# Eleven layers of a first block in three matmul passes instead of one fp32 pass, with later attention splits and another last stretch

## The chip, the cores and the metric

The kernel runs on one core of one Trainium2 chip. The metric is the device time of one execution in microseconds (us). One execution was also taken by the hardware profiler; its span runs from the first to the last instruction. The engines are TensorE (PE, with its weight loads as PEld), VectorE (DVE), ScalarE (ACT), GpSimd (POOL) and SyncE (SP), which issues the transfers. Each engine takes its instructions in the program's order.

## The reference, cut to what matters

```python
for t in range(S):                                    # attention, 4 batches x 8 heads, 768 steps, width 48
    cur = np.einsum('bhd,bhe->bhde', u[None] * kt, vt)
    y[:, :, t] = np.einsum('bhd,bhde->bhe', rt, state + cur)
    state = wt[:, :, :, None] * state + np.einsum('bhd,bhe->bhde', kt, vt)
...
h = x @ w_in                                          # 3072 tokens, 384 -> 2048
x = (h * np.clip(h + 3.0, 0.0, 6.0) / 6.0) @ w_out    # 2048 -> 384
...
xn = x / np.sqrt(np.mean(x * x, axis=-1, keepdims=True) + 1e-06) * rms_g
out = (silu(xn @ w_gate) * (xn @ w_val)) @ w_out2     # 384 -> 1536 -> 384
```

## The kernel before

The 768 steps are cut into six blocks c of 128 steps; a block holds 512 tokens (four batches). For each block there are four attention jobs (one per batch; job j = 4c + b) and the 16 layers f of the first MLP, 128 hidden channels each. The program is a list of steps n, written out by hand. A step holds one `ff1` (a layer's first matmuls, L613) and the `ff2` of two steps earlier (L630). Block 0 has 21 steps: layers 0 to 4 are done in halves of 256 tokens in steps 0 to 9, layers 5 to 15 at the whole width of 512 tokens in steps 10 to 20, so layer f has step f + 5. Block 1 begins with step 21. The lists `before[n]`, `between[n]` and `behind[n]` hold what is emitted ahead of a step's `ff1`, after it, and at its end; this alone sets the order on each engine.

There are two ways to do a layer. In the fp32 way (L444 and L450) one fp32 matmul per 128x128 tile multiplies the unsplit weight and input; the profile shows it as two instructions. In the three-pass way (L438, L467) weight and input each have a high part (fp32r) and a low remainder, and three fp32r matmuls per tile do high x high, high x low of the input, low of the weight x high, in that order (`PASS`). In block 0, layers below `F32_F` = 12 take the fp32 way.

What a three-pass layer needs: `Weight.scale` (ACT L146) and `Weight.bits` (DVE L151 and L152, here the shift and the or) make the fp32 weight in a tile `x` (three buffers); a transfer copies it into its place in `wide_a` (layers 0 to 6) or `wide_b` (7 to 15); `Weight.parts` then writes the high part (ACT L161) and the low part (DVE L162). Behind `ff1`, `emit_act` runs ACT L455 and DVE L456 (the min and multiply, which frees one of two PSUM tiles `hps`, so `ff1` of step n + 2 waits for it), and `emit_split` runs ACT L460 and POOL L461, which reads one of two tiles `a`. In block 0 the parts of x itself (`x_parts`, tile `xt`) are made behind step 15.

An attention job of blocks 1 to 5 is placed by `plan(j, n)`: in step n two scans on DVE (L273) and a product on POOL (`bonus1`, L300 and L301); in n + 1 two DVE products (L296, `muls`), a reduce that waits for POOL (L305) and three small POOL instructions (`decay`); in n + 2 `fill` (eight ACT instructions, L331), the matmuls `aps` and DVE's `choose` (L356, which waits for the fill); in n + 3 the matmuls `yps` (which wait for `choose`), the copy `y` (ACT L398) and eight small transfers x<-y; in n + 5 `split` (ACT L414, POOL L415) into `xt` of the next block. In block 0 the jobs 4, 5, 6, 7 have n = 6, 9, 12, 15, and job 8 has n = 19.

The second MLP follows in three rounds of two blocks. At the very end the loop over `FLUSH` (L1117) gives the last five products e2 to e6 of the last group, one PSUM bank `pe` for all of them, with units F of output matmuls between them; `done` (L837) multiplies each by its gate.

Of the kernel before, what the change touches and what calls it, by code (L numbers as in the profile page):

```python
# [9 lines left out]
F32 = mybir.dt.float32  # L10
# [3 lines left out]
AF = mybir.ActivationFunctionType  # L14
ALU = mybir.AluOpType
# [14 lines left out]
WP = 4 * DM  # L30
NG = F2 // 3
LAGS = (5, 0, 0, 0, 0, 0)
F32_F = 12


@with_exitstack
def kernel(
# [93 lines left out]

    class Weight:
        def __init__(self, src):
            self.src, self.near = src, False

        def load(self):
            self.raw = st_p.tile([128, 2 * DM], U64, tag="raw", name="raw", bufs=3)
# [11 lines left out]
        def bits(self):  # L149
            x = st_p.tile([128, 2 * DM], U32, tag="x", name="x", bufs=3)  # L150
            nc.vector.tensor_scalar(x, self.words()[0], 29, None, ALU.logical_shift_right)  # L151
            nc.vector.scalar_tensor_tensor(  # L152
                out=x, in0=self.mag.bitcast(U32), scalar=3, in1=x, op0=ALU.logical_shift_left, op1=ALU.bitwise_or)
            self.x = x.bitcast(F32).rearrange("p (a n) -> p a n", a=2)
            nc.sync.dma_start(
                out=self.dst[:, :, 1, :].bitcast(U32), in_=x.rearrange("p (a n) -> p a n", a=2))
            if not self.near:
                self.x = self.dst[:, :, 1, :].bitcast(F32)

        def parts(self):  # L160
            nc.scalar.activation(out=self.dst[:, :, 0, :], in_=self.x, func=AF.Copy)  # L161
            nc.vector.tensor_tensor(  # L162
                out=self.dst[:, :, 1, :], in0=self.x, in1=self.dst[:, :, 0, :].bitcast(F32), op=ALU.subtract)


# [371 lines left out]
    def plan(j, n):  # L537

        jb = jobs[j]
        before[n] += [jb.scans, jb.bonus1]  # L540
        before[n + 1] += [jb.muls, jb.bonus2, jb.decay]
        before[n + 2] += [jb.fill]
        between[n + 2] += [jb.pe_a, jb.pe_kt, jb.choose, jb.copy_kt]
        between[n + 3] += [jb.pe_y, jb.pe_u, jb.copy_y, jb.add_u]
        if j + 2 < len(jobs):
            behind[n + 3] += [lambda: jobs[j + 2].load("w", "rk", "v")]
        if j + 1 < len(jobs):
            behind[n + 1] += [lambda: jobs[j + 1].load("rks")]
        before[n + 5] += [jb.split]


    j0, j1, j2, j3 = jobs[:B]
# [22 lines left out]
        if f + 3 < F1:  # L575
            behind[n] += [wa[f + 3].load]
    for f in range(F1):
        before[f + 19 if f < F32_F else f + LAGS[0] - 1] += [wa[f].parts]
    behind[2] += [lambda: jobs[4].load("w", "rk", "rks", "v")]
    behind[4] += [lambda: jobs[5].load("w", "rk", "v")]  # L580

# [6 lines left out]
    for c in range(1, NC_):  # L588
        norm_plan(c, first[c], False)

    def x_parts():
        for k in range(KT):
            h = xts[0][:, k, 0, :]
            nc.scalar.activation(out=h, in_=x0[:, k, :], func=AF.Copy)
            nc.vector.tensor_tensor(out=xts[0][:, k, 1, :], in0=x0[:, k, :], in1=h.bitcast(F32), op=ALU.subtract)

    behind[F32_F + LAGS[0] - 2] += [x_parts]
    acc, norms, todo = None, {}, []


# [41 lines left out]
    def run(fs):  # L642
        for x in fs:
            x()
# [85 lines left out]
    def after(n, *fns):  # L730
        for x in fns:
            queue.append([n, x])
# [27 lines left out]
    class Triple:  # L760
# [76 lines left out]
        def done(self, i, o, ps=None):  # L837
            src = o if ps is None else ps
            self.o[i] = o
            if self.gate is None:  # L840
                nc.scalar.activation(out=o, in_=src, func=AF.Silu)  # L841
                return
            eng = nc.gpsimd if ps is None else nc.vector
            eng.tensor_tensor(out=o, in0=src, in1=self.gate.o[i], op=ALU.mult)  # L844
            f, t = i // 2, i % 2

            def split():
                g = gset(self.j // 2 * 2 + t)[f]
                nc.scalar.activation(out=g[:, 0, :], in_=o, func=AF.Copy)
                nc.gpsimd.tensor_tensor(out=g[:, 1, :], in0=o, in1=g[:, 0, :].bitcast(F32), op=ALU.subtract)  # L850
            after(6 if self.fast else 2, split)

    class Plain(Triple):

# [111 lines left out]
    for f in range(W1):  # L966
        wa[f].dst = wpair[f]
        wa[f].near = f < 2
    run((j0.scans, j0.pairs, j0.pe_bonus, j0.muls, j0.fill, j0.pe_a, j1.scans, j1.pairs, j1.pe_bonus, j1.muls))
    run((j0.choose, j1.fill, j1.pe_a, j0.pe_y0, wa[0].scale, wa[0].bits, wa[3].load, j1.choose, j1.pe_y0))  # L970
    run((j0.copy_y0, wa[1].scale, wa[1].bits, wa[4].load, j1.copy_y0, j2.scans))
# [142 lines left out]
        count += 1  # L1114

    FULL = "b a1 e2 d c1 F F e3 c2 a2 F e4 c3 F F e5 c4 F F e6 c5 F F e1".split()
    FLUSH = "F e2 F e3 F F e4 F F e5 F e6 F F".split()  # L1117
    prev, gate, coming = None, None, None
    fill = ff2_units() + ff2_units()
    for j in range(6 * NG + 1):  # L1120
# [25 lines left out]
        if j < 4:  # L1146
            room = 8 if j else 18
            for i, x in enumerate(cur.units((1, 0) if j == 3 else (0, 1))):
                paced(x)
                if fill and i * room // 18 < (i + 1) * room // 18:  # L1150
                    paced(fill.pop(0))
            assert count == lengths[j]
            continue
        want, n = {4: 7, 5: 7, 6: 6}.get(j, 9), 0
        for u in FULL if cur else FLUSH:
            if u == "F":
# [17 lines left out]
            coming = None  # L1174
        prev = cur
    assert not chores, list(chores)
    for x in fill + out_units(NC_ // 2 - 1, NG - 1, 0, (0, 2, 1)):
        unit(x)
    for x in out_units(NC_ // 2 - 1, NG - 1, 1, (0, 1, 2), None, True):
        unit(x)  # L1180
# [81 lines left out]
```

## Time and profile before

| | |
|---|---|
| time, median of 3 runs | 954.37 us (954.22 to 954.45) |
| the profiled execution: time, span | 955.4 us, 953.6 us |
| PE busy | 932.0 us, 98% of the span |
| DVE, ACT, POOL busy | 641.8, 476.5, 539.8 us |
| block 0 from step 10 to block 1's first matmuls | 72.20 to 135.87 us |
| block 0, PE's begin of step 12 and of step 15 | 81.62 and 101.02 us |
| from step 10 to block 1: PE, DVE, ACT, POOL busy | 63.47, 50.20, 32.45, 22.71 us |

PE is busy almost throughout, so time is gained where PE's own work shrinks, and lost where PE is made to wait.

### The profile page before, as it was taken

How to read it: one execution, taken by the hardware profiler on the slowest of the kernel's cores; microseconds unless marked ns; L12 is line 12 of the kernel's file. 1: busy time of each engine (PE TensorE's matmuls, PEld its weight loads, DVE VectorE, ACT ScalarE, POOL GpSimd, SP SyncE). 2: the span in 40 equal slices, each digit the busy share in tenths (PEclk: the TensorE clock that was granted, in tenths of full speed). 3: DMA queues.
4: the chain of work that ended last, by engine and by line, in shares of the span. 5: the costliest groups of instructions: out<-in, count | busy, mean ns of one | idle time of the engine just before them, and what ended most of it. 6: DMA issues, size and time to landing. Idle time of an engine off the chain costs nothing.

```text
span 953.6 us, 14291 instructions
## 1 busy us (share of the span) xinstructions
PE 932.0 (98%) x5085; PEld 735.8 (77%) x5085; DVE 641.8 (67%) x908; ACT 476.5 (50%) x946; POOL 539.8 (57%) x459
## 2 busy tenths in 40 slices
PE   5899999999999999999999999999999999999998
PEld 4675577778878887777888888787777887888876
DVE  6867776878778787867645377557798557554543
ACT  3544656645655654564554554446545444433331
POOL 0022355766866676774465677579466679235325
PEclk9899999999999999999999999999999999999999
DMA  9687842236654563661662477854699642644321
GB/s 341 217 327 235 282 148 81 83 110 214 201 191 164 169 205 125 214 212 41 232 223 67 153 293 260 293 215 173 202 375 326 257 181 83 248 166 148 151 78 67
DMA packets 63127, 184.77 MB, mean 194 GB/s; under 512 B 8912, under 2 KB 23248, under 8 KB 58448
## 3 DMA queue, kind: packets, MB, share of 16 engines
q1 hardware_dynamic: 63056, 183.87, 54.7%
q8 instruction: 40, 0.66, 0.3%
q14 instruction: 31, 0.25, 0.1%
HBM read 134.29 MB, written 39.32 MB: 182 GB/s over the span
## 4 chain that ended last, share of the span: by engine, by line
PE 88%; DVE 5%; issue 2%; ACT 2%; POOL 1%; DMA 1%; SPq 0%; POOLq 0%; ACTq 0%; DVEq 0%
PE o L467 17%; PE hps L438 16%; PE o L744 14%; PE pe L744 10%; PE pc L744 8%; PE pa L744 4%; PE o L450 3%; PE hps L444 3%; PE pb L744 3%; PE aps L350 2%; PE yps L392 2%; PE pd L744 1%; PE ktp L338 1%; PE yps L386 1%; DVE w L273 1%
## 5 line engine op out<-in xcount | busy, mean ns | idle before, releaser
L461 POOL TENSOR_TENSOR g<-a,g 128x512 fp32r<-128x512 f32 x84 | 116.4, 1385 | 139.8 <-ACT g L460 139.7
L456 DVE SCALAR_TENSOR_TENSOR a<-a,hps 128x512 f32<-128x512 f32 x84 | 57.3, 682 | 83.8 <-ACT a L455 83.6
L467 PE MATMUL o<-g,wide_b 128*128 128x512 f32 x441 | 113.4, 399 | 0.0
L438 PE MATMUL hps<-xt,wide_b 128*128 128x512 f32 x441 | 111.9, 398 | 0.0
L744 PE MATMUL o<-xt,wide_b 128*128 128x512 f32 x405 | 107.5, 395 | 0.0
L455 ACT ACTIVATE a<-hps,half 128x512 f32<-128x512 f32 x84 | 57.4, 683 | 84.1 <-PE hps L438 79.9
L438 PEld LDWEIGHTS hps<-xt,wide_b 128*128 128x128 f32 x441 | 82.7, 187 | 21.2 <-issue 1.0
L467 PEld LDWEIGHTS o<-g,wide_b 128*128 128x128 f32 x441 | 81.2, 188 | 19.5 <-issue 0.5
L460 ACT ACTIVATE g<-a 128x512 fp32r<-128x512 f32 x84 | 53.1, 632 | 80.5 <-DVE a L456 78.8
L744 PEld LDWEIGHTS o<-xt,wide_b 128*128 128x128 f32 x405 | 76.0, 188 | 18.2
L467 PE MATMUL o<-g,wide_a 128*128 128x512 f32 x315 | 78.6, 394 | 0.0
L438 PE MATMUL hps<-xt,wide_a 128*128 128x512 f32 x315 | 77.6, 390 | 0.2 <-POOL xt L415 0.2
L273 DVE TENSOR_TENSOR_SCAN w<-w,dd 128x520 f32<-128x520 f32 x48 | 74.7, 1556 | 4.5 <-DMA w<-in_dram 2.9
L438 PEld LDWEIGHTS hps<-xt,wide_a 128*128 128x128 f32 x315 | 59.0, 188 | 13.3 <-POOL xt L415 0.6
L467 PEld LDWEIGHTS o<-g,wide_a 128*128 128x128 f32 x315 | 58.2, 188 | 12.3 <-issue 0.2
L779 DVE TENSOR_TENSOR q<-pc,q 128x512 f32<-128x512 f32 x80 | 55.1, 688 | 17.8 <-PE pc L744 7.0
L844 POOL TENSOR_TENSOR q<-q,q 128x512 f32<-128x512 f32 x40 | 55.2, 1380 | 14.5 <-DVE q L779 14.3
L331 ACT ACTIVATE a<-iperm,cb 128x128 f32<-128x128 f32 x192 | 58.5, 387 | 0.1
L744 PE MATMUL o<-g,wide_b 128*128 128x512 f32 (+1 forms) x216 | 55.5, 390 | 0.0
L300 POOL TENSOR_TENSOR rks<-rks 128x384 f32<-128x384 f32 x20 | 29.6, 1482 | 42.4 <-DMA rks<-in_dram 37.1
L841 ACT ACTIVATE q<-q 128x512 f32<-128x512 f32 x40 | 25.3, 632 | 51.3 <-DVE q L779 51.3
L844 POOL TENSOR_TENSOR o<-o,o 128x512 f32<-128x512 f32 x10 | 14.1, 1409 | 63.9 <-DVE o L779 63.9
(204 smaller groups left out, 2020.2 us busy)
## 6 DMA issues: line engine op xcount, KB each, us to landing
wraw<-in_dram SPq DMA_DIRECT2D x36, 384.0 KB, 4.0
wide_b<-wo SPq DMA_DIRECT2D x12, 1152.0 KB, 8.0
w<-wd SPq DMA_DIRECT2D x10, 1280.0 KB, 6.0
wide_b<-wd SPq DMA_DIRECT2D x10, 1280.0 KB, 6.0
w<-in_dram SPq DMA_DIRECT2D x24, 520.0 KB, 3.9
rk<-in_dram SPq DMA_DIRECT2D x24, 512.0 KB, 5.1
raw<-in_dram SPq DMA_DIRECT2D x16, 768.0 KB, 7.3
rks<-in_dram SPq DMA_DIRECT2D x20, 384.0 KB, 5.4
```

The lines of the kernel that those rows point to most:

```text
L273: nc.vector.tensor_tensor_scan(out=x, data0=x, data1=dd.rearrange("p a h j -> p (a h j)"), initial=0.0, op0=ALU.mult, op1=ALU.add)
L300: nc.gpsimd.tensor_tensor(out=x, in0=x, in1=self.rks[:, 1, :], op=ALU.mult)
L331: nc.scalar.activation(out=self.head(h), in_=iperm, func=AF.Copy, scale=self.cb[:, h, :])
L438: nc.tensor.matmul(ps, slot[:, l, k * 128:(k + 1) * 128], xt[:, k, r, :], start=(k == 0 and j == 0), stop=(k == KT - 1 and j == 2))
L455: nc.scalar.activation(out=a, in_=ps, func=AF.Relu, scale=1.0 / 6.0, bias=half)
L456: nc.vector.scalar_tensor_tensor(out=a, in0=a, scalar=1.0, in1=ps, op0=ALU.min, op1=ALU.mult)
L460: nc.scalar.activation(out=g[:, 0, :], in_=a, func=AF.Copy)
L461: nc.gpsimd.tensor_tensor(out=g[:, 1, :], in0=a, in1=g[:, 0, :].bitcast(F32), op=ALU.subtract)
L467: nc.tensor.matmul(acc[m][:, cols], slot[:, l, m * 128:(m + 1) * 128], g[:, r, :], start=(first and j == 0), stop=(parts or last and j == ...
L744: nc.tensor.matmul(ps, lhs[:, l, :], rhs[:, r, :], start=first and j == 0, stop=True, skip_group_check=not (first and j == 0))
L779: nc.vector.tensor_tensor(out=out, in0=a, in1=b, op=op)
L844: eng.tensor_tensor(out=o, in0=src, in1=self.gate.o[i], op=ALU.mult)
```

## The change

Layers 5 to 15 of block 0 all take the three-pass way (`F32_F` = 5, seven layers more). Their parts are made from the tile `x`, without the transfer into `wide_a` or `wide_b`, and stand first in a step shortly before the layer's `ff1`; for the layers in `LOW_POOL` the low part is POOL's. The parts of x are made behind steps 6, 7 and 8, the low ones on POOL. An attention job's `split` stands behind its step, but for the last job of a block. In the flush the F units stand two by two ahead of each product, the last ten units of output are taken from one list, and the last gate products are on DVE.

```diff
-F32_F = 12
+F32_F = 5
+LOW_POOL = (5, 6, 7, 9, 11, 13)
...
+            if self.stays:
+                return
             nc.sync.dma_start(
                 out=self.dst[:, :, 1, :].bitcast(U32), in_=x.rearrange("p (a n) -> p a n", a=2))
...
-        def parts(self):
+        def parts(self, pool=False):
             nc.scalar.activation(out=self.dst[:, :, 0, :], in_=self.x, func=AF.Copy)
-            nc.vector.tensor_tensor(
+            (nc.gpsimd if pool else nc.vector).tensor_tensor(
...
-        before[n + 5] += [jb.split]
+        (before if jb.b == B - 1 else behind)[n + 5] += [jb.split]
...
-        before[f + 19 if f < F32_F else f + LAGS[0] - 1] += [wa[f].parts]
+        if f < F32_F:
+            before[f + 19] += [wa[f].parts]
+        else:
+            before[{5: 6, 6: 8, 7: 9, 8: 11}.get(f, f + 4)].insert(0, lambda f=f: wa[f].parts(f in LOW_POOL))
...
-    behind[F32_F + LAGS[0] - 2] += [x_parts]
+    for k in range(KT):
+        behind[6 + k] += [lambda k=k: x_parts(k)]
...
-            eng = nc.gpsimd if ps is None else nc.vector
+            final = self.j == 6 * NG - 1
+            eng = nc.gpsimd if ps is None and not final else nc.vector
...
-            after(6 if self.fast else 2, split)
+            after(4 if final else 6 if self.fast else 2, split)
...
-    FLUSH = "F e2 F e3 F F e4 F F e5 F e6 F F".split()
+    FLUSH = "F F e2 F F e3 F F e4 F F e5 F F e6".split()
...
+        if not cur:
+            fill += out_units(NC_ // 2 - 1, NG - 1, 0, (0, 2, 1))
```

Line numbers shift by 3 to 7 in the changed kernel. On POOL, from job 4's product (L300, L301) to job 5's, there stands before:

```order
L300 TENSOR_TENSOR rks<-rks 128x384
L301 TENSOR_TENSOR rks<-rks,ub 128x384
L288 TENSOR_TENSOR g<-f_109,w 128x4
L289 TENSOR_TENSOR st_104<-st_104,g 128x192
L291 COPY f_109<-w 128x4
L300 TENSOR_TENSOR rks<-rks 128x384
L301 TENSOR_TENSOR rks<-rks,ub 128x384
```

and in the changed kernel, from behind job 4's product (here L303, L304) on:

```order
L600 TENSOR_TENSOR xt<-x_93,xt 128x512
L291 TENSOR_TENSOR g<-f_109,w 128x4
L292 TENSOR_TENSOR st_104<-st_104,g 128x192
L294 COPY f_109<-w 128x4
L600 TENSOR_TENSOR xt<-x_93,xt 128x512
L165 TENSOR_TENSOR wide_a<-x,wide_a 128x2x384
L600 TENSOR_TENSOR xt<-x_93,xt 128x512
L165 TENSOR_TENSOR wide_b<-x,wide_b 128x2x384
L303 TENSOR_TENSOR rks<-rks 128x384
L304 TENSOR_TENSOR rks<-rks,ub 128x384
```

Three low parts of x (128x512) and the low parts of layers 6 and 7 (128x768) stand between the two jobs; layer 5's stands ahead of job 4's product.

On ACT, from the L455 of step 12 to job 6's fill, there stands before:

```order
L455 ACTIVATE g<-hps,half 128x512
L398 ACTIVATE y<-yps 128x512
L146 ACTIVATE mag<-raw 128x768
L455 ACTIVATE g<-hps,half 128x512
L146 ACTIVATE mag<-raw 128x768
L414 ACTIVATE xt<-x 128x3x128
L331 ACTIVATE a<-iperm,cb 128x128 x8
```

and in the changed kernel:

```order
L458 ACTIVATE a<-hps,half 128x512
L463 ACTIVATE g<-a 128x512
L401 ACTIVATE y<-yps 128x512
L147 ACTIVATE mag<-raw 128x768
L164 ACTIVATE wide_b<-x 128x2x384
L458 ACTIVATE a<-hps,half 128x512
L463 ACTIVATE g<-a 128x512
L147 ACTIVATE mag<-raw 128x768
L164 ACTIVATE wide_b<-x 128x2x384
L334 ACTIVATE a<-iperm,cb 128x128 x8
```

Two splits (L463, each behind DVE's min and multiply of its step) and the high parts of layers 9 and 10 stand ahead of the fill now, and job 5's split (L414) stands behind step 14.

On PE, in the flush (`pe` is a product e2 to e6, `pa`, `pb`, `pc` and `o` are F units of three matmuls), there stands before:

```order
L744 MATMUL pe<-wide_b 128x512 x3
L744 MATMUL pa<-xt,wide_b 128x512 x3
L744 MATMUL pe<-wide_b 128x512 x3
L744 MATMUL pa<-xt,wide_b 128x512 x3
L744 MATMUL pe<-wide_a,wide_b 128x512 x3
L744 MATMUL pa<-xt,wide_b 128x512 x3
L744 MATMUL pb<-xt,wide_b 128x512 x3
L744 MATMUL pe<-wide_a,wide_b 128x512 x3
```

and in the changed kernel:

```order
L750 MATMUL pe<-wide_b 128x512 x3
L750 MATMUL pa<-xt,wide_b 128x512 x6
L750 MATMUL pe<-wide_b 128x512 x3
L750 MATMUL pa<-xt,wide_b 128x512 x3
L750 MATMUL pb<-xt,wide_b 128x512 x3
L750 MATMUL pe<-wide_a,wide_b 128x512 x3
```

Two units, where there was one, stand now between each product and the next.

## Rows read from the trace of the kernel before

**Rows 1.** Waits of PE, whole span: total us, times, longest us

```profile
PE yps L386 <- DVE a L356: 1.2, 2, 0.7
...
PE pe L744 <- DVE o L779: 0.6, 2, 0.4
```

**Rows 2.** The chain that ended last: start us, us, what, count

```profile
91.78 2.58 PE o L450 x6
...
195.07 2.10 PE hps L438 x9
...
238.42 2.04 PE o L467 x9
```

**Rows 3.** Timelines of PE and POOL where block 1 begins

```profile
135.87 2.11 PE L438 MATMUL hps<-xt,wide_a 128*128 128x512 f32 x8 [0.20 <-POOL xt L415]
...
134.08 1.73 POOL L415 TENSOR_TENSOR xt<-x,xt 128x384 fp32r<-128x384 f32 x1
```

**Rows 4.** Timeline of DVE in block 1

```profile
168.47 1.24 DVE L273 TENSOR_TENSOR_SCAN w<-w,dd 128x520 f32<-128x520 f32 x1
...
169.99 1.91 DVE L273 TENSOR_TENSOR_SCAN w<-w,dd 128x520 f32<-128x520 f32 x1
171.82 1.98 DVE L162 TENSOR_TENSOR wide_b<-wide_b 128x768 fp32r<-128x768 f32 x1
...
174.32 2.34 DVE L296 TENSOR_TENSOR rk<-rk,w 128x512 f32<-128x512 f32 x2
```

**Rows 5.** Timeline of POOL in the same stretch

```profile
168.89 1.91 POOL L461 TENSOR_TENSOR g<-a,g 128x512 fp32r<-128x512 f32 x1 [2.16 <-ACT g L460]
170.76 2.22 POOL L491 TENSOR_TENSOR sq<-sq 128x512 f32<-128x512 f32 x1
172.95 1.73 POOL L300 TENSOR_TENSOR rks<-rks 128x384 f32<-128x384 f32 x1
174.76 1.36 POOL L301 TENSOR_TENSOR rks<-rks,ub 128x384 f32<-128x384 f32 x1
```

**Rows 6.** Timelines of POOL and DVE in block 0, instructions that ran alone

```profile
79.12 1.00 POOL L415 TENSOR_TENSOR xt<-x,xt 128x384 fp32r<-128x384 f32 x1 [6.01 <-ACT xt L414]
...
118.54 1.27 POOL L461 TENSOR_TENSOR g<-a,g 128x512 fp32r<-128x512 f32 x1 [4.02 <-ACT g L460]
...
116.24 0.96 DVE L162 TENSOR_TENSOR wide_b<-wide_b 128x768 fp32r<-128x768 f32 x1 [0.91 <-ACT wide_b L161]
```

**Rows 7.** Timeline of DVE: L152 of layer 8, L456 of steps 10, 12, 15

```profile
68.21 1.64 DVE L152 SCALAR_TENSOR_TENSOR x<-mag,x 128x768 uint32<-128x768 uint32 x1
...
75.70 0.69 DVE L456 SCALAR_TENSOR_TENSOR g<-g,hps 128x512 f32<-128x512 f32 x1 [0.79 <-ACT g L455]
...
89.30 0.65 DVE L456 SCALAR_TENSOR_TENSOR g<-g,hps 128x512 f32<-128x512 f32 x1
...
106.00 0.66 DVE L456 SCALAR_TENSOR_TENSOR g<-g,hps 128x512 f32<-128x512 f32 x1
```

**Rows 8.** Groups by form, 0 to 160 us: count, busy us, mean ns, idle before

```profile
L460 ACT ACTIVATE g<-a 128x512 fp32r<-128x512 f32 x8 | 5.1, 632 | 10.7 <-DVE a L456 10.7
...
L161 ACT ACTIVATE wide_a<-wide_a 128x768 fp32r<-128x768 f32 x6 | 5.0, 833 | 0.0
...
L594 ACT ACTIVATE xt<-x 128x512 fp32r<-128x512 f32 x3 | 1.7, 624 | 0.0
```

**Rows 9.** Timeline of ACT, just before job 6's fill

```profile
96.44 0.52 ACT L414 ACTIVATE xt<-x 128x384 fp32r<-128x384 f32 x1 [2.39 <-DMA x<-y]
```

**Rows 10.** Timeline of PE, first product and last unit of the flush

```profile
926.02 0.85 PE L744 MATMUL pe<-wide_b 128*128 128x512 f32 x3
...
937.63 6.46 PE L744 MATMUL o<-xt,wide_b 128*128 128x512 f32 x27
...
932.38 1.56 PE L744 MATMUL pb<-xt,wide_b 128*128 128x512 f32 x6
933.78 0.86 PE L744 MATMUL pe<-wide_a,wide_b 128*128 128x512 f32 x3
```

More of the change, by code (lines that the diff above doesn't have):

```diff
@@ L133, in __init__ @@
         def __init__(self, src):
-            self.src, self.near = src, False
+            self.src, self.near, self.stays = src, False, False
         def load(self):
@@ L589, with x_parts @@
         norm_plan(c, first[c], False)
[L591 to L595, printed above, removed]
-    behind[F32_F + LAGS[0] - 2] += [x_parts]
+    def x_parts(k):
+        h = xts[0][:, k, 0, :]
+        nc.scalar.activation(out=h, in_=x0[:, k, :], func=AF.Copy)
+        nc.gpsimd.tensor_tensor(out=xts[0][:, k, 1, :], in0=x0[:, k, :], in1=h.bitcast(F32), op=ALU.subtract)
+    for k in range(KT):
+        behind[6 + k] += [lambda k=k: x_parts(k)]
     acc, norms, todo = None, {}, []
@@ L968 @@
         wa[f].near = f < 2
+    for f in range(F32_F, F1):
+        wa[f].stays = True
     run((j0.scans, j0.pairs, j0.pe_bonus, j0.muls, j0.fill, j0.pe_a, j1.scans, j1.pairs, j1.pe_bonus, j1.muls))
@@ L1176 @@
     assert not chores, list(chores)
-    for x in fill + out_units(NC_ // 2 - 1, NG - 1, 0, (0, 2, 1)):
+    for x in fill:
         unit(x)
```

## The prediction

> **What bounds the kernel now.** The table gives PE 98% busy, and the view of PE's waits says where the rest goes: two waits of `yps` for DVE in block 1, 1.2 us together, and two of the flush's products for DVE, 0.6 us [rows 1]. The reader is to see that almost no wait is left to remove: the time falls only if PE's work falls, and rises wherever PE is made to wait. So I read the chain next for the price of a layer, then the timelines of DVE, POOL and ACT around steps 8 to 21 for what feeds it.
>
> **The change, part by part.**
>
> *PE's own work.* Six fp32 instructions (one `ff1` or `ff2` of a whole layer) take 2.58 us on the chain; nine fp32r ones take 2.10, at some places 2.04 [rows 2]. Seven layers change, so 14 such groups: 14 x 0.48 = 6.7 us less work on PE (14 x 0.54 = 7.6 at most). The Trainium skill, "FP8 and Floating Point Precision", section "TensorE Precision Notes", counts four passes for true fp32; three of four would make the group 1.94 and the sum 9.0 us. The rows show 2.10, since nine weight loads and matmuls don't run at the rate of six, and the rows decide.
>
> *What is added beside PE.* Steps 10 to 16 get a split each (ACT 0.63 [rows 8], POOL 1.27 [rows 6]). The parts of layers 5 to 11 move from block 1 into block 0: seven high parts on ACT (0.83 each [rows 8]), two low parts on DVE (0.96 [rows 6]) and five on POOL, with layer 13's a sixth; x's three low parts leave DVE for POOL. POOL has no 128x768 row: 384 columns take 1.00 and 512 take 1.27 [rows 6], so 768 lie between 1.27 and 2.0; I take 1.8, on the line through the two.
>
> *What POOL and DVE do to each other.* In block 1 both have a queue of work, and there the reader is to see that they take turns. The scan from 168.47 ends at 169.71; POOL's L461, begun at 168.89, ends at 170.80, 1.09 after it; DVE's second scan, begun at 169.99, ends at 171.90, 1.10 after that; POOL's next at 172.98, 1.08 later; DVE's low part at 173.80, 0.82 later; POOL's rks at 174.68, 0.88 later [rows 4, 5]. Each ends its own lone time [rows 6], less some 0.15, after the other's end. So a two-input DVE instruction that meets a POOL one waits it out: up to 1.1 for a 512-wide one, 0.9 for a 384-wide one and, by the same 0.15, some 1.65 for a 768-wide one. The Trainium skill, "SBUF — State Buffer", section "SBUF: two separate sides", says that the two engines share a port pair as an exclusive lock held for the whole instruction. Held whole, the some 14 collisions counted below would cost 0.15 each, 2 us, more; I keep the rows' holds.
>
> *Steps 8 to 10.* On ACT a high part of x and layer 6's high part come ahead of job 4's fill: 0.62 + 0.83 [rows 8], 1.3 when run back to back. `choose` waits for that fill, and DVE goes on with layer 8's shift and or and job 5's two scans, while POOL now has x's last low part, layer 7's and job 5's product (first order piece). In turns these cost DVE 1.05, 1.65, 0.85 and 0.6. From 1.3 + 4.1 = 5.4 go the 0.79 that DVE waits at step 10 before, the 0.7 by which layer 8's or is already late there (1.64, where a lone two-input instruction of its size takes 0.96 [rows 6]), and some 0.4 of gaps: step 10's L456, at 75.70 before [rows 7], is 3.5 us later. The hps tile of step 9 comes free as late, and step 11's `ff1` waits some 1 us.
>
> *Steps 10 to 12.* A split, layer 8's high part and POOL's split beside job 6's scans: 0.8 us more than the 13.6 between 75.70 and 89.30 [rows 7].
>
> *Steps 12 to 15.* From L456 of step 12 to that of step 15 before takes 106.00 - 89.30 = 16.7 us [rows 7]. It holds a 2.39 wait for x<-y [rows 9], which the later `split` takes off the path to the fill, and gets two splits and two high parts on ACT (second order piece): 2 x 0.63 + 2 x 0.83 = 2.9 [rows 8]. Alone that is 17.2. Then come DVE's turns with POOL: layer 11's or behind a split 1.1, a `muls` behind layer 9's low part 1.65, layer 13's shift and or behind a split and job 5's `xt` 0.65 + 0.85, job 7's scans behind layer 11's low part 1.65 and the product 0.6: 6.5, of which some 2 lie beside ACT's copy, scale and high part. 17.2 + 4.5 = 21.7, 5.0 more. PE's three steps would be 16.5 (the table's 101.02 - 81.62 = 19.4 before, less 6 groups x 0.48), so PE waits: step 14 for layer 9's low part, which stands behind step 12's late L456, its split, the copy y, a scale and the high part; `yps` of jobs 5, 6 and 7 for `choose`; step 17 for layer 12's parts.
>
> *Steps 15 to 21.* No more POOL parts but layer 13's: 0.4. Block 1's first matmuls wait for job 7's `xt`, as before: POOL's 1.73 there [rows 3] may be 1.0, 0.7 less. Sum: 3.5 + 0.8 + 5.0 + 0.4 - 0.7 = 9.0 us later than 135.87 [rows 3], PE's saving swallowed. That is the upper end, every turn lost. The lower: without any collision (before's own gone too) my count along the same instructions has `xt` ready near 133.4, 2.5 us earlier. Rows 4 and 5 show turns lost whenever both queues hold work, and POOL's does from step 6 on, but a microsecond's shift makes some miss: I take three quarters of the way, +6.1.
>
> *Block 1.* Layers 5 to 11 have no parts there any more, and job 8's split is behind its step. The two waits of `yps` (1.2 [rows 1]) go: DVE's choose of job 9 came behind two high and two low parts. -1.2, bounds 0 and -1.5.
>
> *Flush.* From the first product to the end of the 15 units 937.63 - 926.02 = 11.6 us pass; a unit is (933.78 - 932.38) / 2 = 0.70 [rows 10], 15 are 10.5. The 1.1 over is PE waiting for DVE to read the one bank `pe`. Two units, 1.4 us, then cover DVE's read (third order piece); the gate product moved to DVE follows the read and lies beside the same units. -1.1, bounds 0 and -1.1.
>
> *At nothing.* Eleven transfers less: only SP and DMA have less to do, which can bring loads earlier, and PE waits for none of them. That `x` is held until its low part is done delays `bits` of layer 12 behind layer 9's, beside the wait of step 14. Splits behind steps in blocks 2 to 5: PE has no wait there to lose [rows 1].
>
> Total: +6.1 - 1.2 - 1.1 = +3.8. The profiled execution took 955.4 us, so 959.2 by it; it lies 1.0 above the median of the runs, 954.37, and against that the forecast is 958.2.
>
> **Rivals.** (a) *PE stays the bound in block 0*: DVE and POOL have slack in sum (50.20 and 22.71 busy of 63.7 us), and PE never waits there before. Against it: the chain of steps 12 to 15 alone, 17.2, already exceeds PE's 16.5. It would give 954.4 - 6.7 - 1.2 - 1.1 = 945.4. (b) *The chain binds, but collisions mostly fall into waits*: 954.4 - 2.5 - 2.3 = 949.6. This is the other side, and it decides from where fewer than about 40% of the collision time reaches the chain: break-even is +2.3 of a span from -2.5 to +9.0. (c) *Half of it reaches the chain*: +3.2 - 2.3, about 955.3, no change. (d) All of it: +9.0 - 2.3, 961.1, and 963 with the skill's full holds.
>
> **How the numbers follow.** A measurement of this kernel can tell about 0.2%, 1.9 us, from no change. Forecast with (d), slower by more than that: 0.53; (c) within it: 0.16; (b) 0.18 and (a) 0.13, both faster: 0.31. The forecast's own range is 954.5 to 963. The range for 8 in 10 reaches into (a): 946.5 to 963, leaving out some 0.1 below and less than 0.1 above.
>
> **What would show it.** Right: the 14 changed groups of `ff1` and `ff2` at 2.1 us; L456 of step 10 near 79 and of step 15 near 113; DVE's scans and shifts at 1.6 to 2.3 in block 0; PE waiting on a low part at steps 14 and 17 and on `choose` at steps 12, 15 and 18; block 1 beginning after 138; no wait of `yps` in block 1; no gaps in the flush. Wrong: block 1 beginning before 135.9, with L456 of step 15 at or before 106; or POOL's 768-wide low part well under 1.6; or DVE's instructions at their lone times beside POOL's.

## The result, and the profile after

The changed kernel is slower: 965.5 us median (963.7 to 967.1, six executions) against 954.3 (953.1 to 954.7, six), ratio 1.0116, 95% interval 1.0102 to 1.0129. The forecast was 958.2 with a range up to 963.0: the sign was right, the size was not. The profiled execution took 963.72 us, span 961.9, so 8.3 more than the span before.

The page's first part (busy us, share of the span, instructions):

```profile
PE 929.4 (97%) x5127; PEld 744.8 (77%) x5127; DVE 644.4 (67%) x904; ACT 478.9 (50%) x953; POOL 562.5 (58%) x470
```

PE is busy 2.6 us less, not 6.7 (the slow groups below take most of it back), and it stands idle for 32.5 us (21.6 before). The waits over the whole span (total us, times, longest us):

```profile
PE yps L389 <- DVE a L359: 4.7, 4, 2.3
...
PE hps L441 <- POOL xt L418: 2.4, 1, 2.4
PE hps L441 <- ACT wide_b L164: 2.1, 1, 2.1
...
PE hps L441 <- POOL wide_b L165: 1.2, 1, 1.2
```

Of [rows 1], the two waits of `yps` in block 1 are gone. In their place stand waits of block 0: `yps` four times for `choose`, `ff1` for a low part (POOL), for a high part (ACT) and, at block 1's head, 2.4 us for `xt` (two smaller ones, 0.9 for DVE's min and multiply at step 11 and 0.7 for ACT's part of `xt`, are not shown). The reader is to see next where they come from, in the timeline of DVE (start us, us, instruction), beside [rows 7]:

```profile
77.65 0.67 DVE L459 SCALAR_TENSOR_TENSOR a<-a,hps 128x512 f32<-128x512 f32 x1
...
92.06 0.66 DVE L459 SCALAR_TENSOR_TENSOR a<-a,hps 128x512 f32<-128x512 f32 x1
...
93.48 2.09 DVE L153 SCALAR_TENSOR_TENSOR x<-mag,x 128x768 uint32<-128x768 uint32 x1
95.49 2.94 DVE L299 TENSOR_TENSOR rk<-rk,w 128x512 f32<-128x512 f32 x2
...
109.52 2.73 DVE L276 TENSOR_TENSOR_SCAN w<-w,dd 128x520 f32<-128x520 f32 x1
...
112.53 1.64 DVE L276 TENSOR_TENSOR_SCAN w<-w,dd 128x520 f32<-128x520 f32 x1
114.09 0.66 DVE L459 SCALAR_TENSOR_TENSOR a<-a,hps 128x512 f32<-128x512 f32 x1
```

The min and multiply (L459) of steps 10, 12 and 15 begin at 77.65, 92.06 and 114.09, where they began at 75.70, 89.30 and 106.00. Between steps 12 and 15 pass 22.0 us (16.7 before). The rows between are what the turns with POOL make of them: the or (L153) takes 2.09 for a lone 0.96, the two products 2.94 for 1.28, the scans 2.73 and 1.64 for 1.24. POOL's 128x768 low part, of which there was no row, takes 1.82:

```profile
93.46 1.30 POOL L464 TENSOR_TENSOR g<-a,g 128x512 fp32r<-128x512 f32 x1 [2.42 <-ACT g L463]
95.47 1.82 POOL L165 TENSOR_TENSOR wide_b<-x,wide_b 128x768 fp32r<-128x768 f32 x1 [0.71 <-ACT wide_b L164]
```

What this does to PE, in its timeline:

```profile
85.57 0.67 PE L389 MATMUL yps<-rk,st 64*64 64x128 f32 x16 [2.29 <-DVE a L359]
...
88.17 3.35 PE L470 MATMUL o<-g,wide_a 128*128 128x512 f32 x9
...
97.34 1.89 PE L441 MATMUL hps<-xt,wide_b 128*128 128x512 f32 x7 [1.16 <-POOL wide_b L165]
...
117.47 4.08 PE L441 MATMUL hps<-xt,wide_b 128*128 128x512 f32 x9 [2.08 <-ACT wide_b L164]
...
132.20 2.26 PE L441 MATMUL hps<-xt,wide_b 128*128 128x512 f32 x9
134.30 2.26 PE L470 MATMUL o<-g,wide_b 128*128 128x512 f32 x9
...
144.36 3.26 PE L441 MATMUL hps<-xt,wide_a 128*128 128x512 f32 x8 [2.43 <-POOL xt L418]
147.55 1.56 PE L353 MATMUL aps<-rk 48*128 48x128 f32 x16
```

A layer's nine matmuls take 2.10 from start to start (132.20, 134.30), as in [rows 2], so PE did save its 6.7 us (on seven layers: four of the title's eleven had three passes before); but it waits 2.29, 1.16, 2.08 and 2.43 at these rows, and block 1's `xt` is there at 144.36, where [rows 3] has 135.87. And three groups take 3.35, 4.08 and 3.26 us, where the same work takes 2.1 to 2.3. The windows around two of them (PEclk is the granted clock):

```profile
core 0: us, PE busy (x) PEld busy (x) DVE busy (x) ACT busy (x) POOL busy (x), PEclk, DMA share, GB/s
118.00:120.00 2.00, 2.00 (x6) 1.25 (x5) 2.00 (x5) 0.00 (x0) 0.45 (x1) 0.50 0.16 45
144.00:146.00 2.00, 1.64 (x5) 1.36 (x6) 0.05 (x1) 1.92 (x6) 1.92 (x5) 0.75 0.94 336
146.00:148.00 2.00, 2.00 (x8) 1.15 (x9) 0.18 (x1) 2.00 (x6) 0.42 (x1) 0.50 0.87 340
148.00:150.00 2.00, 2.00 (x22) 1.79 (x21) 2.00 (x4) 1.00 (x3) 0.00 (x0) 0.90 0.04 17
```

After its waits PE works for some 3 us at a granted clock of 0.50, the lower of its two levels (1.2 of 2.4 GHz). No step of the prediction had that.

In the flush, the stretch of [rows 10]:

```profile
934.95 0.85 PE L750 MATMUL pe<-wide_b 128*128 128x512 f32 x3
...
943.82 0.96 PE L750 MATMUL pe<-wide_a,wide_b 128*128 128x512 f32 x3 [0.22 <-DVE q L785]
...
946.73 5.76 PE L750 MATMUL o<-xt,wide_b 128*128 128x512 f32 x24
```

From product e1 to the last run of units pass 11.78 us with 16 groups of 0.70 (11.2) in them, 0.6 over; before it was 1.1 over. One wait is left, 0.22 for the DVE instruction that reads the bank.

Two sums close the account. Where a kernel's job 4 begins its first `yps` (67.95 here, 68.73 before) varies by chance: 67.95 and 68.81 in two profiles of the changed kernel, and in all profiles below between 67.0 and 69.7, with no order by kernel. So I count from there to block 2's first `aps` (251.13 and 242.43): 183.2 us now, 173.7 before, **9.5 more**, of which 9.3 up to block 1's `xt`. With 0.8 less ahead of it and 0.5 less in the flush that is 8.2 of the span's 8.3. This stretch, called **the block stretch** below, is the finest measure of a kernel here.

### The profile page after: what moved, and what is told of

Its sections match the earlier page's. It is cut to its first block, busy times and chain, and to the rows that moved or that the text cites. A ratio compares the mean times of both kernels' runs of the same rounds, so it can differ in the third digit from the quotient of the medians.

```text
span 961.9 us, 14350 instructions
## 1 busy us (share of the span) xinstructions
PE 929.4 (97%) x5127; PEld 744.8 (77%) x5127; DVE 644.4 (67%) x904; ACT 478.9 (50%) x953; POOL 562.5 (58%) x470
## 4 chain that ended last, share of the span: by engine, by line
PE 85%; DVE 6%; issue 3%; ACT 3%; POOL 1%; DMA 1%; SPq 0%; POOLq 0%; DVEq 0%; ACTq 0%
PE o L470 18%; PE hps L441 17%; PE o L750 14%; PE pe L750 10%; PE pc L750 8%; PE pa L750 4%; PE pb L750 3%; PE aps L353 2%; DVE w L276 2%; PE yps L395 2%; PE pd L750 1%; PE ktp L341 1%; PE yps L389 1%; ACT a L334 1%; PE hps L447 1%
## 5 line engine op out<-in xcount | busy, mean ns | idle before, releaser
L464 POOL TENSOR_TENSOR g<-a,g 128x512 fp32r<-128x512 f32 x91 | 125.7, 1382 | 157.6 <-ACT g L463 151.5
L459 DVE SCALAR_TENSOR_TENSOR a<-a,hps 128x512 f32<-128x512 f32 x91 | 62.0, 681 | 109.6 <-ACT a L458 108.3
L441 PE MATMUL hps<-xt,wide_b 128*128 128x512 f32 x486 | 124.4, 400 | 3.2 <-ACT wide_b L164 2.1
L470 PE MATMUL o<-g,wide_b 128*128 128x512 f32 x486 | 125.0, 400 | 0.0
L458 ACT ACTIVATE a<-hps,half 128x512 f32<-128x512 f32 x91 | 62.2, 684 | 102.7 <-PE hps L441 98.5
L441 PEld LDWEIGHTS hps<-xt,wide_b 128*128 128x128 f32 x486 | 91.7, 189 | 27.0 <-ACT wide_b L164 2.7
L463 ACT ACTIVATE g<-a 128x512 fp32r<-128x512 f32 x91 | 57.6, 633 | 102.5 <-DVE a L459 100.4
L470 PEld LDWEIGHTS o<-g,wide_b 128*128 128x128 f32 x486 | 89.3, 188 | 21.3 <-issue 0.5
L441 PE MATMUL hps<-xt,wide_a 128*128 128x512 f32 x333 | 83.7, 396 | 4.0 <-POOL xt L418 2.4
L470 PE MATMUL o<-g,wide_a 128*128 128x512 f32 x333 | 84.2, 398 | 0.0
L851 POOL TENSOR_TENSOR q<-q,q 128x512 f32<-128x512 f32 x36 | 50.0, 1390 | 13.6 <-DVE q L785 13.3
L750 PEld LDWEIGHTS o<-g,wide_b 128*128 128x128 f32 x216 | 40.0, 188 | 9.4
L299 DVE TENSOR_TENSOR rk<-rk,w 128x512 f32<-128x512 f32 x48 | 46.4, 1005 | 0.1
```

The source lines that it names most:

```text
L299: nc.vector.tensor_tensor(out=x, in0=x, in1=s[:, :, :, 0:HF], op=ALU.mult)
L441: nc.tensor.matmul(ps, slot[:, l, k * 128:(k + 1) * 128], xt[:, k, r, :], start=(k == 0 and j == 0), stop=(k == KT - 1 and j == 2))
L458: nc.scalar.activation(out=a, in_=ps, func=AF.Relu, scale=1.0 / 6.0, bias=half)
L459: nc.vector.scalar_tensor_tensor(out=a, in0=a, scalar=1.0, in1=ps, op0=ALU.min, op1=ALU.mult)
L463: nc.scalar.activation(out=g[:, 0, :], in_=a, func=AF.Copy)
L464: nc.gpsimd.tensor_tensor(out=g[:, 1, :], in0=a, in1=g[:, 0, :].bitcast(F32), op=ALU.subtract)
```

## The experiments

The kernel before ran beside each set of kernels on the same chip (954.1 to 954.9 us median); ratios are to it.

**1. The two small parts of the change alone.** The kernel before with the new `FLUSH`, the last gate product on DVE and the last units in one list; then the same with

```diff
-        before[n + 5] += [jb.split]
+        (before if jb.b == B - 1 else behind)[n + 5] += [jb.split]
```

> The kernel before with the end order alone (the flush in pairs of units, the last gate product on DVE, its split two units earlier, the last output units in the flush). Prediction's term: two waits of the flush go, 1.1 us less, 953.2. By the trace of the changed kernel the stretch from the flush's first product to the end shortened by only 0.5, so 953.8. Rival: the end order is part of the loss; then it is above 954.3.

> The kernel before with the end order and with the attention splits behind their steps, block 0 with its eleven fp32 layers. Theory (all of the loss is block 0's chain of ACT, DVE and POOL under the added parts): within 0.5 of the run with the end order alone, PE still without a wait over 1 us in block 0. Rival: the later splits themselves make PE wait for xt at the head of block 1 and elsewhere; then 1 to 3 us slower than the end order alone.

Measured: 953.89 us, 0.9993 (0.9984 to 1.0002), and 953.87, 0.9996 (0.9988 to 1.0005); block stretches 173.0 and 173.5. In the trace of the first kernel the 16 groups from product e1 on take 11.77 us, 0.6 over, as in the changed kernel; so by the trace the end order is worth 0.5. The time alone, 0.7 less with an interval from 1.5 less to 0.2 more, can't tell 0.5 from 1.1. Of the later splits the runs show no cost. What is left for the loss is the rest of the change: block 0's new layers, with the parts made for them and for x.

**2. The changed kernel without POOL's parts.** POOL's low parts of x, of six layers and of block 0's g are left out; matmuls read the high part instead.

```diff
-                    ps, slot[:, l, k * 128:(k + 1) * 128], xt[:, k, r, :],
+                    ps, slot[:, l * wl, k * 128:(k + 1) * 128], xt[:, k, r * xl, :],
...
-        nc.gpsimd.tensor_tensor(out=g[:, 1, :], in0=a, in1=g[:, 0, :].bitcast(F32), op=ALU.subtract)
+        if c:
+            nc.gpsimd.tensor_tensor(out=g[:, 1, :], in0=a, in1=g[:, 0, :].bitcast(F32), op=ALU.subtract)
```

> The changed kernel without POOL's parts: POOL makes no low parts of x, of layers 5, 6, 7, 9, 11 and 13, and none of block 0's g; the matmuls read the high part in their place, as many as before. Theory (turns of DVE and POOL make the loss, and low parts that come late): the cycle from step 12's min and multiply to step 15's falls from 22.0 to 17.2 or less, block 1 begins some 10 us earlier (134 to 135 for 144.4), and the time is 951 to 955. Rival (the work added on ACT and DVE themselves is the chain, turns matter little): the cycle stays at 20 or more and the time at 960 or more.

Measured: 950.87 us, 0.9961 (0.9946 to 0.9976), block stretch 170.0. DVE's timeline, where a line's number is up to one higher:

```profile
89.92 0.66 DVE L460 SCALAR_TENSOR_TENSOR a<-a,hps 128x512 f32<-128x512 f32 x1
...
91.34 0.96 DVE L153 SCALAR_TENSOR_TENSOR x<-mag,x 128x768 uint32<-128x768 uint32 x1
92.22 1.28 DVE L300 TENSOR_TENSOR rk<-rk,w 128x512 f32<-128x512 f32 x2
...
103.92 1.24 DVE L277 TENSOR_TENSOR_SCAN w<-w,dd 128x520 f32<-128x520 f32 x1
...
106.60 0.66 DVE L460 SCALAR_TENSOR_TENSOR a<-a,hps 128x512 f32<-128x512 f32 x1
```

From step 12 to step 15 16.7 us, the cycle of before; the or takes 0.96, the products 1.28 and the scan 1.24 again. The rival falls: ACT's seven high parts and seven splits, which are still there, don't bind. What binds is the making of the low parts, by DVE's turns with it and where PE waits for one.

**3. The same parts on DVE.** Would DVE do better alone?

```diff
-LOW_POOL = (5, 6, 7, 9, 11, 13)
+LOW_POOL = ()
...
-            g = emit_split(a, n)
+            g = emit_split(a, n, None, nc.gpsimd if c else nc.vector)
```

(and x's low parts on DVE)

> The changed kernel with all low parts of block 0 (x, layers 5 to 13, g) on DVE: no POOL parts to take turns with, but DVE does 0.66 to 0.96 us more work for each and stands still for ACT's high part ahead of each, some 0.8. Theory (the added work costs the chain that much wherever it stands, since DVE is the chain): the cycle from step 12 to step 15 stays at 20 to 23 us, two low parts and three splits at 1.5 to 1.8 each on 16.7, less 2 to 3 of its idle time, and the time at 959 to 966. Rival (the turns alone make the loss, DVE has room in its idle time): cycle near 17 to 18, time 952 to 955.

Measured: 961.47 us, 1.0073 (1.0057 to 1.0088), block stretch 180.7. From step 12 to 15:

```profile
90.98 0.66 DVE L459 SCALAR_TENSOR_TENSOR a<-a,hps 128x512 f32<-128x512 f32 x1
...
112.89 0.67 DVE L459 SCALAR_TENSOR_TENSOR a<-a,hps 128x512 f32<-128x512 f32 x1
```

21.9 us, the same as with POOL. Without the turns with these parts (those with the attention's products on POOL stay) DVE pays its own work and its stand for each high part; the block stretch is 2.5 us shorter, by other steps. The added low parts cost the chain about as much wherever they stand.

**4. PE's clock.** Matmuls that nobody reads fill PE's waits, so that only the clock changes: first at five places, then at the three where nothing makes the filling wait.

```diff
+    def idle(ps, n):
+        for i in range(n):
+            nc.tensor.matmul(ps, wpair[5][:, 0, 0, 0:128], xts[0][:, 0, 0, :], start=True, stop=True)
...
+            idle(ps, {(0, 9): 4, (0, 12): 7, (1, 0): 10}.get((c, f), 0))
             emit_h(wpair[f][:, 0], xts[c][:, :, :, cols], ps)
```

> The changed kernel with 35 more matmuls on PE, 128x512 fp32r of 0.23 us each, whose results nobody reads, put where PE waits in block 0: 8 and 6 ahead of yps in steps 12 and 15, 4, 7 and 10 ahead of ff1 of steps 14, 17 and 21; ACT, DVE and POOL have their order unchanged. Theory (the granted clock falls to the lower level after PE's waits over 2 us, and this lengthens the path): the granted clock stays at 1.00 from 84 to 150 us, the three slow groups (3.35, 4.08, 3.26 us) become 2.1 to 2.3, and the time falls by 2.5 to 4 us, to 960 to 961.5, with no runs near 967. Rival (the slow matmuls lie beside the chain of ACT, DVE and POOL, which comes as late anyway): within 1 us of the changed kernel's 964 to 967.

> The changed kernel once more, unchanged, as a control beside the next three on one chip, and for a profile of the longer of its two groups of times (964 and 967). 963.7 to 967; if the profile is of the longer group, the theory of the clock expects another stretch at the lower granted clock behind a wait of PE, and no other difference in block 0; the rival expects the time in start-up or in transfers.

> As the run with filled waits, without the two fills ahead of yps, which themselves waited for ACT's copy of k and came 2 us late: 4, 7 and 10 matmuls nobody reads ahead of ff1 of steps 14, 17 and 21. Theory (only the fall of the clock at block 1's head is exposed, the two ahead of it lie in time in which PE waits later anyway): PE at full clock from 114 to 150, 1 to 2 us less than the changed kernel's shorter group, 962 to 963, and no runs near 967. Rival (it costs nothing): 964 and 967 as the control.

Measured: 964.12 us with five fills, 1.0103 (1.0089 to 1.0116); 964.53 for the changed kernel again, 1.0108 (1.0094 to 1.0123); 962.58 with three fills, 1.0087 (1.0073 to 1.0101), block stretch 181.8. The first misses its 960 to 961.5: two fills stood 2.1 and 1.4 us behind ACT's copy of k and came late, and its times lie with the changed kernel's shorter ones. But its granted clock stays at 1.00 from 66 to 180 us, and its block stretch is 181.7, 1.5 shorter; its profiled execution began job 4's `yps` late, at 69.52. The second filled kernel, at block 1's head:

```profile
141.08 2.46 PE L542 MATMUL hps<-xt,wide_a 128*128 128x512 f32 x10
...
144.88 2.14 PE L441 MATMUL hps<-xt,wide_a 128*128 128x512 f32 x8 [1.11 <-POOL xt L418]
146.94 1.16 PE L353 MATMUL aps<-rk 48*128 48x128 f32 x16
```

`xt` comes 76.5 us after job 4's `yps`, as in the changed kernel (76.4), so block 0 is as late; but the eight matmuls take 2.14, not 3.26, and the next group 1.16, not 1.56. That is 1.5 of clock, and the block stretch is 1.4 shorter, as the theory had it. The slow groups ahead of it cost nothing, since PE waits again behind them: the second kernel has its clock at 0.50 from 86 to 89 us, behind a wait of 2.34 at step 12 that it doesn't fill, the first never, and their block stretches are the same. Here the rival was right.

The clock also splits the times. The changed kernel's ten timed executions, control included, fall into six of 963.7 to 964.7 us at a mean granted clock of 0.992 or 0.993 and four of 966.5 to 967.1 at 0.988 or 0.989. The eight executions with fills are at 0.994 to 0.998, and none is over 964.4. No trace shows the longer group (the control's is of the shorter), so what its PE does is argued from the next run.

**5. Two added layers instead of seven.** `F32_F = 10`.

> The changed kernel with only layers 10 and 11 of block 0 in three passes beside the four that already were (parts ahead of steps 14 and 15, layer 11's low part on POOL, x's three on POOL in steps 6 to 8), ten layers in fp32. Theory (the gain on PE is kept only while the chain of ACT and DVE has slack, and two layers' parts fit into the slack of 19.4 against 16.7): PE saves 4 groups of 0.48, 1.9, and part of block 1's 1.2 of waits goes, end order 0.7: 951 to 953. Rival (any part in block 0 makes the chain bind): 955 to 957.

Measured: 957.19 us, 1.0033 (1.0020 to 1.0045), block stretch 177.6. That is near the rival's number, and not by its reason. PE waits nowhere in block 0 but at its end:

```profile
133.45 0.50 PE L441 MATMUL hps<-xt,wide_a 128*128 128x512 f32 x1 [0.21 <-ACT xt L417]
136.38 3.78 PE L441 MATMUL hps<-xt,wide_a 128*128 128x512 f32 x8 [2.43 <-POOL xt L418]
140.09 2.08 PE L353 MATMUL aps<-rk 48*128 48x128 f32 x16
142.10 1.11 PE L341 MATMUL ktp<-ident,rk 128*128 128x128 f32 x4
142.87 3.62 PE L470 MATMUL o<-g,wide_b 128*128 128x512 f32 x9
```

and there, in the windows (columns as above):

```profile
134.00:136.00 2.00, 0.00 (x0) 0.00 (x0) 1.84 (x2) 0.70 (x2) 2.00 (x2) 0.86 1.01 363
136.00:138.00 2.00, 1.62 (x4) 1.33 (x5) 0.07 (x1) 1.90 (x6) 1.92 (x5) 0.50 0.96 304
144.00:146.00 2.00, 2.00 (x7) 1.56 (x6) 0.96 (x1) 0.58 (x1) 0.00 (x0) 0.58 0.00 0
```

`xt` comes 67.9 us behind job 4's `yps` (67.1 before), though PE is there 1.6 earlier; it waits 2.43, and then runs at the lower level for some 9 us. Its groups take 3.78, 2.08, 1.11 and 3.62 us for 2.11, 1.16, 0.66 and 2.35: 4.3 us for the clock alone. Before, PE came 0.2 ahead of `xt` [rows 3], and its granted clock stayed at 1.00 there.

**6. Job 7's split earlier.** From ahead of step 20 to ahead of step 19, with five, ten, nine and eight layers in fp32 (the last three are `F32_F` = 10, 9, 8):

```diff
+        if j == 2 * B - 1:
+            before[n + 4] += [jb.split]
```

> The changed kernel with one split moved: job 7's (the last part of block 1's xt) ahead of step 19 in place of step 20. Theory (block 1 waits for xt only because that split stands on ACT and POOL behind step 19's min and multiply, which DVE comes to last; x itself lies ready some 7 us earlier): the waits of 0.67 and 2.43 at block 1's head go, and with them the stretch at the lower clock behind them, 1.2 to 1.5: 4.3 to 4.6 less, 959.5 to 960.5, no runs near 967. Rival (DVE is the chain there, and the next instruction behind it comes as late): 962 or more.

> As the run with two layers (10 and 11) added in three passes, and job 7's split ahead of step 19. Theory (that run's whole loss lies at block 1's head: 2.6 us of wait for xt and some 4 us of PE at half clock behind it): both go, 957.2 less 6 to 7, 950 to 951.5, faster than the kernel before by 0.3 to 0.45%. Rival (the parts in block 0 bind elsewhere too): 953 or more.

> The same with layer 9 in three passes too (parts of layers 9 to 11 in block 0). Theory of slack (PE's three steps 12 to 15 take 18.9, the chain 16.7 and one more high part and low part, some 19): 0 to 1 less than with ten, 949.5 to 951. Rival (each added pair of turns binds at once): 2 or more above the run with ten.

> The same with layer 8 in three passes too (parts of layers 8 to 11 in block 0). By the slack: PE's steps 12 to 15 then 17.5 to 18 against a chain of 19 to 20, so 1 to 3 us above the run with nine, 951 to 954. Rival (PE stays the bound, the turns fall beside its work): 948.5 to 949.5.

Measured: 965.26 us, 1.0116 (1.0102 to 1.0130); 957.06, 1.0025 (1.0014 to 1.0036); 958.16, 1.0033 (1.0020 to 1.0045); 960.28, 1.0056 (1.0044 to 1.0068). The block stretches are 183.7, 176.5, 176.6 and 179.3. My theory fell. At block 1's head PE now waits for DVE's min and multiply in place of `xt`, 1.99, 2.32, 2.64 and 2.32 us; with ten layers:

```profile
136.30 3.90 PE L441 MATMUL hps<-xt,wide_a 128*128 128x512 f32 x9 [2.32 <-DVE a L459]
```

And x does not lie ready: ACT, sent to the split early, stands for it, as its timeline in the first of these shows, and SP's of the changed kernel shows why.

```profile
131.70 0.63 ACT L463 ACTIVATE g<-a 128x512 fp32r<-128x512 f32 x1 [2.75 <-DVE a L459]
132.24 0.58 ACT L401 ACTIVATE y<-yps 128x512 f32<-128x512 f32 x1
...
139.25 0.53 ACT L417 ACTIVATE xt<-x 128x384 fp32r<-128x384 f32 x1 [5.70 <-DMA x<-y]
```

```profile
133.27 0.52 SPq L404 DMA_DIRECT2D x<-y  x1
...
135.75 2.49 SPq L407 DMA_DIRECT2D x<-y  x4
```

The eight transfers x<-y go out one by one, 0.52 to 0.59 each, until 138.2, and each lands 1.7 to 2.0 after its issue. In the first of the four runs x is there at 139.25, 6.4 us behind y. So `xt` is late because y is, and y because ACT copies it behind a split that waited 2.75 for DVE. The slack theory fell with it: with ten layers 957, not 951. With nine the block stretch is the same as with ten and PE waits 0.6 at most in block 0; with eight it is 2.7 longer, and PE waits 1.2 for a high part again.

**7. y first.** In step 18 ACT copies job 7's y ahead of the step's split, and job 7's split stays early; five, ten, nine and twelve layers in fp32.

```diff
+            if (c, f) == (0, 13):
+                late.append(lambda: todo.append((c, f, cols, emit_split(a, n), wpair[f][:, 1])))
+                return
...
         run(between[n])
+        while late:
+            late.pop()()
```

> The changed kernel with job 7's split ahead of step 19 and, new, ACT's copy of job 7's y ahead of step 18's split instead of behind it. Theory (y's place is what makes x late): x is there 2.5 to 2.8 us earlier, block 1's ff1 starts without a wait over 0.7 near 141.5 and at full clock; 964 to 965 becomes 959.5 to 961. Rival (DVE's queue: ff1 then waits for step 19's min and multiply, or yps for choose, as long): 963 or more.

> The same two moves with layers 10 and 11 in three passes and ten in fp32 (957.1 with the early split alone, 2.32 of wait and a stretch at half clock at block 1's head). Theory: 4 to 5 less, 952 to 953.5, below the kernel before. Rival: 955 or more.

> The same with layers 9, 10 and 11 in three passes. Without a wait over 0.7 in block 0 in the run with the early split alone; theory: 0.5 to 1 below the run with ten, 951.5 to 953. Rival: above it by 1 or more.

> The same two moves with no added layer in three passes (twelve in fp32 as before; end order and later splits of the change kept; x's parts on POOL in steps 6 to 8): a control for what the moves give by themselves. PE never waits over 0.2 there, so 953.5 to 954.3, as the end order with the later splits (953.9). If it is as fast as the runs with ten and nine, the three-pass layers bring nothing.

Measured: 963.63 us, 1.0091 (1.0077 to 1.0106); 957.24, 1.0023 (1.0015 to 1.0032); 956.26, 1.0006 (0.9995 to 1.0017); 956.18, 1.0015 (1.0007 to 1.0024). The wait at block 1's head is gone with five and nine layers, 0.61 with ten. But `yps` of the next job now waits for `choose`, 3.07, 3.25 and 2.91 us, and 2.09 with twelve. In the run with nine layers:

```profile
142.49 0.67 PE L389 MATMUL yps<-rk,st 64*64 64x128 f32 x16 [2.91 <-DVE a L359]
```

The wait moved on, as the rival said. With twelve layers no work is saved and there was no such wait, and the moves, with the low parts of x and layer 13 on POOL, cost 2 us against run 1 (956.2 for 953.9), where none was expected: ACT and POOL stand at the early split, 5.05 and 5.04 us.

**8. The split behind job 8's products.** Still ahead of step 19, but last there; nine and ten layers in fp32, y first.

```diff
+    before[19] += [jobs[2 * B - 1].split]
```

> As the run with nine layers in fp32 and y first, with job 7's split at the end of what stands ahead of step 19 (behind job 8's products on POOL and layer 0's high part on ACT) instead of at its beginning. Theory (the stalled queues behind the early split made the 2.9 us wait of yps): no wait over 1 us in block 1, full clock from 60 to 200, one group of times, 951 to 953, faster than the kernel before. Rival (DVE has no slack there at any order): a wait over 2 us again, 955 to 957.

> The same place of the split with ten layers in fp32. Theory: 952 to 954, a single group. Rival: 955 to 958 as with the split at the beginning.

Measured: 954.05 us, 0.9991 (0.9981 to 1.0001), and 953.41, 0.9987 (0.9979 to 0.9996); block stretches 174.2 and 172.5. The first is from the longest of its eleven executions (956.3), in which PE waits 2.25 for `choose` and then runs at the lower clock; the theory, no wait over 1 us, failed there. The second is the fastest kernel of the study that leaves no part out, by 0.13% faster than before, but its interval overlaps that of the end order alone (0.9993), so the layers on three passes are not shown to bring anything. `choose` of job 8 still comes late, in the second:

```profile
142.36 0.67 PE L389 MATMUL yps<-rk,st 64*64 64x128 f32 x16 [1.91 <-DVE a L359]
```

```profile
139.41 0.96 DVE L165 TENSOR_TENSOR wide_a<-wide_a 128x768 fp32r<-128x768 f32 x1 [3.78 <-ACT wide_a L164]
...
140.88 1.33 DVE L359 COPY_PREDICATED a<-mask,aps 128x512 f32<-128x512 uint32 x2
```

It stands on DVE behind a low part of block 1, which waits 3.78 for ACT's high part, itself behind a fill. PE is ahead of DVE there, and waits 1.91. Counted from job 4's `yps`, `choose` began at 72.1 before and begins at 73.1 here; PE came to its `yps` at 75.0 before and comes at 72.7 here. Most of what PE had saved is waited away.

## Why the prediction was right in sign and wrong in size

**Right.** PE's own saving is 2.10 for 2.58 as priced. Between the named points, counted from job 4's `yps`, the terms of the upper end came near: L459 of step 10 2.7 later (3.5 was said), step 12 0.8 (0.8), step 15 5.3 (5.0), block 1's `xt` 0.4 (0.4, less 0.7 for a turn that stayed: POOL's L418 takes 1.70 as before). That their sum fits as well as it does, 9.3 for 9.0, is partly luck: 0.8 too much in steps 8 to 10, where DVE's four turns cost 3.4 and not 4.15, stands against 0.3 too little behind step 12 and the 0.7. The turns between steps 12 and 15 add 1.13 + 1.66 + 0.22 + 1.42 + 1.49 + 0.40 = 6.3 to DVE's rows; the prediction had 6.5. A POOL low part takes 1.82 (1.8 was chosen). PE waits at steps 11, 12, 14, 15, 17 and 18, at step 11 0.9 (some 1 was said), at step 17 for the high part and not the low one. The lower end fits too: without POOL's parts (run 2) `xt` is there 64.5 us behind job 4's `yps`, 2.6 earlier than before (2.5 was said for no collision at all). Block 1's two waits of `yps` are gone: from `xt` to block 2's `aps` 106.8 for 106.6 us, with 1.5 of lower clock in it, so 1.3 less (1.2 was said).

**The step that failed** is "but a microsecond's shift makes some miss: I take three quarters of the way, +6.1". It is the whole way: 9.3 by the rows, 9.0 by the sum. No share of the turns is missed by chance: in the control `xt` comes 76.5 us behind job 4's `yps` (76.4 in the first profile), and in the filled kernels, in which PE's work is moved against the others', the same within 0.2. That a queue which is late meets the same partner all the same, since the engines wait for each other, is my reading of this; no run moved one queue alone by a microsecond. This is 3.2 of the error.

**The term that was missing** is the clock: 1.5 at block 1's head in the profiled execution (run with three fills), and perhaps more in the longer group of executions. The prediction read "PE waits" as so many us; here several waits of 2 us and more were followed by 3 to 9 us at half clock.

**A size** was off in the flush: 0.5 instead of 1.1, since 0.6 stays between the units. The prediction took the whole 1.1 for PE waiting for DVE, and the 0.6 of [rows 1] for the flush; but only 0.15 of that lies there, and the other wait, 0.4, lies between 600 and 700 us and is still there.

Together, on the profiled execution: 959.2 predicted, + 3.2 + 1.5 + 0.6, - 0.8 for a start that came earlier by chance: 963.7, as measured. On the median two more lie on top: 1.8, since three of the six executions are of the longer group, and the 1.0 by which the profiled execution of before was above its median. The range ended at 963.0 because its upper end was every turn lost (961.1), or 963 with each turn held whole, with no price for what PE's waits do to its clock.

**Rivals.** (a) and (b), both faster, fall, and so does (c), 955.3: chain and turns bind, and even without POOL's parts (run 2) the time is 950.9, where (b) said 949.6 and (a) 945.4. (d), all of it, is what happened, with 1.5 and the longer group on top.

**What stays open.** That the longer group of the changed kernel is a longer stretch at the lower clock is argued (mean granted clock, none with fills, the 9 us stretch of run 5), not seen in a trace of it. One set of times speaks against it as the only reason: with job 7's split early and five layers in fp32 (run 6), an execution of 967.6 us has a mean clock of 0.993 and one of 964.3 has 0.991. What the eleven transfers saved was not tried alone; no PE wait is ascribed to them before or after.

## What to carry to other kernels

A profile with PE at 98% can hide a chain with no slack: here `xt` came 0.2 us behind PE before the change, and whatever PE saved in block 0 came back as a wait at the next point where another engine is met. So before pricing work taken off the busiest engine, find for each stage the first instruction that it takes from another engine and how early that one is. When two engines take turns over a long stretch, count every turn that the order gives, not a share of them; and price a new wait of PE with the clock that may follow it.

## What the hardware showed that was not expected

- Behind a wait PE's granted clock may fall to the lower level, and this is not the same in every kernel or execution. In block 0 and 1 it fell behind waits of 2.08, 2.29 and 2.43 us in the changed kernel and of 2.43 in run 5; it stayed at 1.00 behind 1.64 (changed kernel), 1.91 (last run), 2.08 and 3.07 (five layers, y first) and 2.91 (nine layers, y first). So the length of the wait does not settle it. Nor does the kernel: in the control, the same program as the changed kernel, it stayed behind step 12's wait of 2.34 and fell at step 14, behind two of 1.34 and 1.15:

```profile
86.44 0.67 PE L389 MATMUL yps<-rk,st 64*64 64x128 f32 x16 [2.34 <-DVE a L359]
...
98.23 3.33 PE L441 MATMUL hps<-xt,wide_b 128*128 128x512 f32 x7 [1.15 <-POOL wide_b L165]
```

  With nine layers and y first, six executions at a mean clock of 0.993 took 956.2 to 957.1 us, five at 0.998 952.9 to 954.5, and one at 0.996 956.5. The Trainium skill, "TensorE: Matmul & The Clock Gate", section "Part 1: The HAM clock gate", says that the clock is halved when PE has been idle and released by activity, and that the moment of the release varies from run to run; the rows agree in kind (0.50 behind waits, 1.00 again some 3 to 9 us later).
- DVE and POOL took turns in the changed kernel's block 0 as in block 1 before: the or begun at 93.48 beside POOL's split of 93.46 (to 94.76) ends at 95.57, 0.81 later, its lone 0.96 less 0.15, the same 0.15 as in [rows 4, 5].
- Eight small transfers from one engine's queue took 6.4 us from y to x, 5.0 of it their issue one after the other (133.27 to 138.24 in the changed kernel).
